# The opening of a fused recurrence and two-layer kernel in the order of one table: three plain blocks, the first two side by side

## The chip, the cores and the metric

The kernel runs on one core of one Trainium2 chip. The metric is the device time of one execution in microseconds (us), lower is better. Every run quoted here, of every kernel, was in the fast state, with a mean granted TensorE clock (the share of full speed that the profile lists) of 0.99 or more, so all of them may be compared. The time of a run is 1.7 to 1.9 us longer than the span of its profile (2.2 to 3.2 in the kernel turn_dve below), so times are set against times and spans against spans.

## The reference

A gated recurrence along the sequence is followed, for each token, by two matrix products with an elementwise function between them.

```python
# x, f_logit: (4, 6080, 256) float32, w_in: (256, 2048) and w_out: (2048, 256) float64
sig = 1 / (1 + np.exp(-f_logit))
f = lower_bound + (1 - lower_bound) * sig
for t in range(6080):                       # per batch row and channel
    h = f[:, t] * h + (1 - f[:, t]) * x[:, t]
    y[:, t] = h
x = y.reshape(24320, 256)
h = x @ w_in
out = ((h - np.tanh(h)) @ w_out).astype(np.float32)
```

The weights arrive as 64-bit floats. The kernel takes the words apart with integer operations and builds fp32 numbers ("rounding a weight", seven steps on VectorE and ScalarE). For small h, h - tanh(h) is a polynomial in h². A guard collects how large h became, and one branch at the end would run a slower fallback, `general()`; with these data it is skipped.

## The kernel before

The 24320 tokens are cut into blocks. The first blocks are "plain": ordinary fp32 matmuls, 32 of 128x512 and 64 of 128x256 for 512 tokens. All later blocks use seven products in place of eight for each 2x2 cut of a matrix product. For these, sums of the weight quarters and of the input quarters must exist first. In the steady part a fixed word list `around` puts the instructions of three neighbouring blocks into each engine's queue, and each engine works its queue off in that order (x_early below shows a wait that comes of it). Matmuls write into banks of PSUM, here of 128x512 fp32 numbers; a bank is free again when its content has been read.

```python
sizes = [TB] + [HB] * (N % TB // HB) + [TB] * (N // TB - 1)   # 512, 256, then 46 x 512
PLAIN = 1 + N % TB // HB                                      # 2: 512 and 256 are plain

def turn(j, s):                      # VectorE: tokens x channels -> channels x tokens
    nc.vector.transpose(
        out=dst[:, 0:n].rearrange("p j k b -> p (j k b)"),
        in_=nats[j, s][:, 0:n, :].rearrange("p j c -> p (j c)"))
def recur(j, k): ...                 # VectorE: tensor_tensor_scan of 128 channels

def to_float32(dsts, raw, temps): ...   # VectorE e, m, r, e, w; ScalarE r, e; all at once

def plain_first(j, u):               # first layer, a quarter u of the 2048 features
    # per half s: 4 matmuls into two PSUM banks (A A, then B D), ScalarE: square, quadratic,
    # VectorE: factor, two products that read the banks
def plain_second(j, u): ...          # second layer into banks Qa, Qb (or Qc)

# ... the opening, in this order in every queue
for step in REC:                     # the whole recurrence of block 0
    steps[step](0)
fetch(1)
ready(0)                             # rounds w_in of quarter 0
for u in range(NU):
    plain_first(0, u)
    for i in {0: (1, 2), 1: (3, 4), 2: (5, 6), 3: (7,)}[u]:
        ready(i)                     # rounds the next weights, two at a time
    if u > 0:
        plain_second(0, u - 1)
    for step in REC[3 * u : 3 * u + 3]:
        steps[step](1)
# ... the same for block 1, with sum_weight() between
bank = ps_b.tile([P, 2, HB], FP32, name="B", tag="B")
nc.tensor.matmul(bank[:], lhsT=zeros[:, 0:P], rhs=zeros[:], ...)   # "the dummy"
for cycle in range(PLAIN, NBLK + 3):
    for name, u, at in turns: ...    # the seven-product part
```

The **dummy**, a matmul of zeros, stands where the plain part ends and the seven-product part begins. I call that place the seam.

Of the kernel before, what the change touches and what calls it, by code (L numbers as in the profile page):

```python
# [7 lines left out]

# [8 lines left out]
P = 128  # L17
# [13 lines left out]
def kernel(  # L31
# [37 lines left out]
    assert D == 2 * P and DFF == 4 * TB and N % HB == 0  # L69


    sizes = [TB] + [HB] * (N % TB // HB) + [TB] * (N // TB - 1)
    PLAIN = 1 + N % TB // HB
# [12 lines left out]
    zeros = const.tile([P, TB], FP32, name="zeros")  # L86



    def fetch_w_in(u, raw, queue):  # L90

        src = moe_w_in.rearrange(
            "(i k a) (s u f) -> i k u a s f", i=G, k=KC, a=H, s=2, u=NU
        )
        dst = raw.rearrange("p (k s f) -> p k s f", k=KC, s=2)
        for i in range(G):
            for k in range(KC):
                queue.dma_start(out=dst[i * H : (i + 1) * H, k], in_=src[i, k, u])
# [8 lines left out]
    def to_float32(dsts, raw, temps):  # L107




        hi = raw.bitcast(INT32).rearrange("p (n c) -> p n c", c=2)[:, :, 1]
        lo = raw.bitcast(UINT32).rearrange("p (n c) -> p n c", c=2)[:, :, 0]
        e, m, r = [t.rearrange("p a b c -> p (a b c)") for t in temps]
        nc.vector.tensor_scalar(
            out=e.bitcast(INT32), in0=hi, scalar1=20, scalar2=0x7FF,
            op0=ALU.logical_shift_right, op1=ALU.bitwise_and,
        )
        nc.scalar.activation(out=r, in_=lo, func=AF.Copy, scale=2.0**-32)
        nc.scalar.activation(  # L120
            out=e.bitcast(INT32), in_=e.bitcast(INT32), func=AF.Relu,
            scale=float(1 << 23), bias=-896.0 * (1 << 23),
        )
        nc.vector.tensor_scalar(
            out=m.bitcast(INT32), in0=hi, scalar1=0xFFFFF, scalar2=0x100000,
            op0=ALU.bitwise_and, op1=ALU.bitwise_or,
        )
        nc.vector.tensor_tensor(out=r, in0=r, in1=m.bitcast(INT32), op=ALU.add)
        nc.vector.scalar_tensor_tensor(
            out=e.bitcast(INT32), in0=hi, scalar=-(1 << 31), in1=e.bitcast(INT32),  # L130
            op0=ALU.bitwise_and, op1=ALU.bitwise_or,
        )
        for dst, view in dsts:
            nc.vector.scalar_tensor_tensor(
                out=dst, in0=view(r), scalar=2.0**-20, in1=view(e),
                op0=ALU.mult, op1=ALU.mult,
            )

    def recurrence(ctx):
# [6 lines left out]
        def fetch(j):  # L146
            t0, nb = starts[j], sizes[j]
            for s in range(2):
                nat = natpool.tile([P, TB // H, KC * H], FP32, name=("fn", "xn")[s])
                src = srcs[s][t0 : t0 + nb, :].rearrange(  # L150
                    "(j b) (i c) -> i b j c", b=H, i=G
                )
                for i in range(G):
                    nc.sync.dma_start(
                        out=nat[i * H : (i + 1) * H, 0 : nb // H, :], in_=src[i]
                    )
                nats[j, s] = nat

        def turn(j, s):
# [5 lines left out]
                in_=nats[j, s][:, 0:n, :].rearrange("p j c -> p (j c)"),  # L165
# [57 lines left out]
        return fetch, steps, ys  # L223

    @with_exitstack
    def fast(ctx):
# [8 lines left out]
        fetch, steps, ys = recurrence(ctx)  # L235
# [17 lines left out]
        raws = {}  # L253

        def fetch_weight(n, queue):
            kind, u = n
            raw = rawpool.tile([P, KC * TB], INT64, name="raw")
            (fetch_w_in, fetch_w_out)[kind](u, raw[:], queue)
            raws[n] = raw

        def round_weight(n):
            kind, u = n
            raw = raws.pop(n)
            temps = [
                rawpool.tile([P, 2, 2, HB], FP32, name=s, tag=s, bufs=1)[:] for s in "emr"
            ]
            w = (w_in, w_out)[kind][u]
            if kind == 0:
                dsts = [(w[:, 0:4, :].rearrange("p n f -> p (n f)"), lambda a: a)]
            else:  # L270
                dsts = [
                    (
                        w[:, 2 * s + k, :].rearrange("p (n a) -> p n a", a=H),
                        lambda t, s=s, k=k: t[:, s * TB : (s + 1) * TB].rearrange(
                            "p (n k a) -> p n k a", k=2, a=H
                        )[:, :, k],
                    )
                    for s in range(2)
                    for k in range(2)
                ]  # L280
            to_float32(dsts, raw[:], temps)

        def sum_weight(n):
            kind, u = n
            w = (w_in, w_out)[kind][u]
            A21 = S3
            for o, a, b, op in (
# [3 lines left out]
                (S3, A11, A21, ALU.subtract),  # L291
            ):
# [174 lines left out]
        def give(j):  # L467
            n = sizes[j] // H
            osb = opool.tile([P, TB // H, KC, H], FP32, name="osb", tag="osb")
            nc.vector.transpose(  # L470
                out=osb[:, 0:n].rearrange("p j k a -> p (j k a)"),
# [7 lines left out]
            for i in range(G):  # L479
                nc.sync.dma_start(  # L480
                    out=dst[i],
                    in_=osb[i * H : (i + 1) * H, 0:n].rearrange("b j k a -> b j (k a)"),
# [61 lines left out]
        def plain_first(j, u):  # L544

            nb = sizes[j]
            n = j * NU + u
            gT = hpool.tile([P, 2, 2, TB], FP32, name="h", tag="h")
            st[n] = gT
            for s in range(2):  # L550
                banks = []
                for c in range(2):
                    pool, name = ((ps_a, "A"), (ps_b, "B" if c == 0 else "D"))[s]
                    bank = pool.tile([P, TB], FP32, name=name, tag=name)
                    banks.append(bank)
                    for k in range(KC):
                        nc.tensor.matmul(  # L557
                            bank[:, 0:nb],
                            lhsT=w_in[u][:, 2 * k + s, c * P : (c + 1) * P],
                            rhs=ys[j][:, k, 0:nb],  # L560
                            start=(k == 0),
                            stop=(k == KC - 1),
                        )
                t, q = [
                    tpool.tile([P, 2, TB], FP32, name=name, tag=name)[:, :, 0:nb]
                    for name in "tq"
                ]
                for c in range(2):
                    nc.scalar.activation(
                        out=t[:, c], in_=banks[c][:, 0:nb], func=AF.Square  # L570
                    )
                nc.scalar.activation(out=q, in_=t, func=AF.Square, scale=RA, bias=RB)
                nc.vector.scalar_tensor_tensor(  # L573
                    out=q, in0=q, scalar=RC, in1=t, op0=ALU.add, op1=ALU.mult
                )
                for c in range(2):
                    nc.vector.tensor_tensor(  # L577
                        out=gT[:, s, c, 0:nb], in0=banks[c][:, 0:nb], in1=q[:, c],
                        op=ALU.mult,
                    )  # L580
                junk = sumpool.tile([P, 2, TB], BF16, name="junk", tag="junk")
                nc.scalar.activation(
                    out=junk[:, :, 0:nb], in_=t, func=AF.Relu, bias=-TINY,
                    accum_out=flags[:, 2 * n + s : 2 * n + s + 1],
                )

        def plain_second(j, u):

            nb = sizes[j]
            ns = nb // P  # L590
            gT = st.pop(j * NU + u)
            if u == 0:
                acc[j] = [
                    ps_b.tile([P, 2, D], FP32, name=f"Q{b}", tag=f"Q{b}")
                    for b in ("ab" if j == 0 else "c")[0 : (ns + 1) // 2]
                ]
            for s in range(2):
                for c in range(2):
                    for i in range(ns):
                        nc.tensor.matmul(  # L600
                            acc[j][i // 2][:, i % 2].rearrange("p (k m) -> p k m", k=2),
                            lhsT=gT[:, s, c, i * P : (i + 1) * P],
                            rhs=w_out[u][:, 2 * s : 2 * s + 2, c * P : (c + 1) * P],
                            start=(u == s == c == 0 and i % 2 == 0),
                            stop=(u == NU - 1 and s == c == 1),
                            skip_group_check=True,
                        )
            if u == NU - 1:
                osb = opool.tile([P, NQ, D], FP32, name="osb", tag="osb")
                for i in range(ns):  # L610
                    nc.scalar.copy(
                        out=osb[:, i].rearrange("p (i k a) -> p k i a", k=2, a=H),
                        in_=acc[j][i // 2][:, i % 2].rearrange(
                            "p (k i a) -> p k i a", k=2, a=H
                        ),
                    )
                nc.sync.dma_start(
# [218 lines left out]
```

## Time and profile before

| | before |
|---|---|
| median of four runs | 2373.88 us (2373.49 to 2375.92) |
| span of the traced run | 2374.0 us |
| first matmul on the recurrence's output | 25.0 us |
| TensorE idle in the first 100 us | 40.4 us |
| TensorE idle from 1000 to 2000 us | 0 |

The head of the page of the kernel before gives each engine's busy time, its share of the span and its instructions:

```profile
span 2374.0 us, 28606 instructions
...
PE 2316.8 (98%) x10628; PEld 2020.9 (85%) x10628; DVE 2130.6 (90%) x2456; ACT 1801.3 (76%) x2685; POOL 2.5 (0%) x8
```

The 57 us in which TensorE (PE) is not busy are 2.4% of the span, nearly all in the first 150 us and in the last 12. So nearly all that order can gain lies in the opening, and the gain is bounded. The start of VectorE's (DVE) timeline of the kernel before (start, duration, engine, line, operation, output and inputs, count, and in brackets the idle time before and who ended it) shows what stands in the way:

```profile
14.63 1.25 DVE L163 STREAM_TRANSPOSE xT<-xn 128x1024 f32<-128x1024 f32 x1 [3.84 <-DMA xn<-in_x_dram]
...
18.81 1.22 DVE L207 TENSOR_TENSOR_SCAN y<-f,v 128x512 f32<-128x512 f32 x1
19.96 0.67 DVE L115 TENSOR_SCALAR e<-raw 128x1024 int32<-128x1024 int32 x1
```

VectorE waits 3.84 us for x, finishes the recurrence at 20.0, and only then touches a weight that ScalarE had begun to convert at 13.16. The queue's order, not the data, makes the weight late.

### The profile page before, as it was taken

The numbers are of one execution on the slowest core, as the hardware profiler recorded it, in microseconds if no ns is written. First come the engines' busy times: TensorE is split into PE (matmuls) and PEld (weight loads), VectorE is DVE, ScalarE is ACT, GpSimd is POOL, SyncE is SP. The second block draws the span as 40 slices with busy tenths as digits, with TensorE's granted clock in tenths as the row PEclk, the third lists the DMA queues.
The fourth block names the chain that finished last, engine by engine and source line by source line (L and its number), as shares of the span: only waits on it lengthen the run. The fifth ranks groups of instructions, "written<-read, shape, count | busy, mean of one in ns | idle before, by whom it ended". The sixth has DMA issues, their size and how long they took to land.

```text
span 2374.0 us, 28606 instructions
## 1 busy us (share of the span) xinstructions
PE 2316.8 (98%) x10628; PEld 2020.9 (85%) x10628; DVE 2130.6 (90%) x2456; ACT 1801.3 (76%) x2685; POOL 2.5 (0%) x8
## 2 busy tenths in 40 slices
PE   4999999999999999999999999999999999999997
PEld 2678888888888888888888888888888888888886
DVE  5888999899999999899989999899989999999987
ACT  4678777877777777777787777777787777777775
POOL 0000000000000000000000000000000000000000
PEclk9999999999999999999999999999999999999999
DMA  5321111211121111211121111111121112111101
GB/s 115 80 48 28 36 27 27 45 36 27 27 43 29 36 27 30 42 36 27 27 45 34 30 27 36 36 36 27 27 45 36 27 27 41 32 36 27 27 9 29
DMA packets 303669, 85.06 MB, mean 36 GB/s; under 512 B 298656, under 2 KB 299424, under 8 KB 303520
## 3 DMA queue, kind: packets, MB, share of 16 engines
q1 hardware_dynamic: 302752, 82.09, 16.9%
q8 instruction: 85, 1.39, 0.3%
q10 hardware_dynamic: 640, 1.05, 0.2%
q14 instruction: 64, 0.52, 0.1%
q0 software_dynamic: 128, 0.00, 0.0%
HBM read 58.20 MB, written 24.90 MB: 35 GB/s over the span
## 4 chain that ended last, share of the span: by engine, by line
PE 95%; DVE 2%; DMA 1%; ACT 1%; issue 0%; SPq 0%; DVEq 0%
PE A L350 26%; PE Qd L433 13%; PE Qb L433 13%; PE Qa L433 13%; PE D L350 13%; PE Qc L433 7%; PE B L350 7%; PE A L557 1%; DMA raw<-in_moe_w_in_dram 1%; PE Qb L600 0%; PE Qa L600 0%; DVE q L573 0%; DVE w_out L293 0%; PE D L557 0%; PE B L557 0%; DVE h L577 0%
## 5 line engine op out<-in xcount | busy, mean ns | idle before, releaser
L350 PE MATMUL A<-T,w_in 128*128 128x256 f32 x2208 | 559.2, 379 | 2.0 <-ACT r L362 1.8
L350 PEld LDWEIGHTS A<-T,w_in 128*128 128x128 f32 x2208 | 419.4, 190 | 59.7 <-ACT r L362 2.2
L394 DVE TENSOR_TENSOR h<-h,q 128x1024 f32<-128x1024 f32 x368 | 437.3, 1219 | 3.2
L388 DVE SCALAR_TENSOR_TENSOR q<-q,t 128x1024 f32<-128x1024 f32 x368 | 439.7, 1216 | 0.0
L381 ACT ACTIVATE q<-t 128x1024 f32<-128x1024 f32 x368 | 382.7, 1052 | 45.3 <-DVE h L394 42.4
L378 ACT ACTIVATE t<-h 128x1024 f32<-128x1024 f32 x368 | 388.6, 1056 | 4.8 <-DVE h L365 2.0
L399 ACT ACTIVATE junk<-t 128x1024 bf16<-128x1024 f32 x368 | 388.1, 1055 | 1.5
L413 DVE TENSOR_TENSOR Tg<-h 128x1024 f32<-128x1024 f32 x368 | 347.9, 945 | 6.5
L433 PE MATMUL Qb<-h,w_out 128*128 128x256 f32 x1472 | 347.7, 379 | 0.0
L433 PEld LDWEIGHTS Qb<-h,w_out 128*128 128x128 f32 x1472 | 279.7, 190 | 38.0
L433 PE MATMUL Qa<-Tg,w_out 128*128 128x256 f32 x736 | 218.9, 379 | 0.0
L433 PE MATMUL Qd<-h,w_out 128*128 128x256 f32 x736 | 218.9, 379 | 0.0
L433 PE MATMUL Qa<-h,w_out 128*128 128x256 f32 x736 | 218.9, 379 | 0.0
L433 PE MATMUL Qd<-Tg,w_out 128*128 128x256 f32 x736 | 218.9, 379 | 0.0
L362 ACT COPY h<-B 128x512 f32<-128x512 f32 x184 | 107.1, 582 | 144.8 <-PE B L350 94.9
L362 ACT COPY h<-A 128x512 f32<-128x512 f32 x184 | 107.3, 583 | 136.5 <-PE A L350 125.2
L365 DVE TENSOR_TENSOR h<-D,r 128x512 f32<-128x512 f32 x184 | 126.8, 689 | 90.7 <-PE D L350 89.7
L365 DVE TENSOR_TENSOR h<-A,r 128x512 f32<-128x512 f32 x184 | 126.2, 686 | 77.2 <-PE A L350 43.4
L350 PE MATMUL D<-T,w_in 128*128 128x256 f32 x736 | 189.1, 379 | 3.0 <-DVE T L320 1.6
L350 PE MATMUL A<-y,w_in 128*128 128x256 f32 x736 | 188.9, 379 | 0.0
L350 PE MATMUL B<-y,w_in 128*128 128x256 f32 x736 | 188.9, 379 | 0.0
L350 PE MATMUL D<-y,w_in 128*128 128x256 f32 x736 | 188.9, 379 | 0.0
(81 smaller groups left out, 2982.2 us busy)
## 6 DMA issues: line engine op xcount, KB each, us to landing
fn<-in_f_logit_dram SPq DMA_DIRECT2D x188, 128.0 KB, 3.1
xn<-in_x_dram SPq DMA_DIRECT2D x188, 128.0 KB, 3.3
out_dram<-osb SPq DMA_DIRECT2D x184, 128.0 KB, 2.8
raw<-in_moe_w_out_dram SPq DMA_DIRECT2D x8, 512.0 KB, 5.2
raw<-in_moe_w_in_dram SPq DMA_DIRECT2D x24, 128.0 KB, 3.4
raw<-in_moe_w_in_dram ACTq DMA_DIRECT2D x8, 128.0 KB, 5.0
out_dram<-osb SPq DMA_DIRECT2D x1, 512.0 KB, 3.0
fn<-in_f_logit_dram SPq DMA_DIRECT2D x4, 64.0 KB, 4.1
```

What stands on the lines that cost most here:

```text
L350: nc.tensor.matmul(ps[:, c], lhsT=w_in[u][:, slot, c * P : (c + 1) * P], rhs=mixes[j][right], start=start and c == 0, stop=True, skip_grou ...
L362: nc.scalar.copy(out=dst, in_=piece(n, bank))
L365: nc.vector.tensor_tensor(out=piece(n, "h")[:, q], in0=piece(n, bank), in1=piece(n, r), op=ALU.add)
L378: nc.scalar.activation(out=half(n, i, "t"), in_=half(n, i), func=AF.Square)
L381: nc.scalar.activation(out=half(n, i, "q"), in_=half(n, i, "t"), func=AF.Square, scale=RA, bias=RB,)
L388: nc.vector.scalar_tensor_tensor(out=q, in0=q, scalar=RC, in1=t, op0=ALU.add, op1=ALU.mult)
L394: nc.vector.tensor_tensor(out=h, in0=h, in1=q, op=ALU.mult)
L399: nc.scalar.activation(out=junk[:, :, :, 0 : st[n]["hb"]], in_=t, func=AF.Relu, bias=-TINY, accum_out=flags[:, 2 * n + i : 2 * n + i + 1],)
L413: nc.vector.tensor_tensor(out=o, in0=a, in1=b, op=ALU.subtract)
L433: nc.tensor.matmul(acc[j, part][:, r, 0 : st[n]["hb"]], lhsT=w_out[u][:, slot, c * P : (c + 1) * P], rhs=piece(n, right)[:, q, c], start=( ...
L557: nc.tensor.matmul(bank[:, 0:nb], lhsT=w_in[u][:, 2 * k + s, c * P : (c + 1) * P], rhs=ys[j][:, k, 0:nb], start=(k == 0), stop=(k == KC - 1),)
```

## The change

The intent is to shorten the opening. It has five parts, and some small ones.

- **Order by a table.** Every step of the opening is a word in one long string; the string's order is each engine's order. Rounding is spread in single steps.
- **Blocks.** Block 2 becomes plain too (512, 256, 512), and blocks 0 and 1 run side by side.
- **Turned by TensorE.** Blocks 0 and 1 are transposed by TensorE against an identity matrix; they then load in rows of 1 KB instead of 256 bytes.
- **Half a weight first.** The first 1 MB of w_in comes in two halves, each rounded alone.
- **Even and odd channels** are the two halves of the 256, in place of blocks of 32. A load of w_in then needs two transfers instead of eight, and VectorE's transposes read or write with a step of 8 bytes.
- **Small ones**, which no run here takes apart: three matmuls of zeros at the very start (TensorE is busy with them from 1.47 us for 5.49 us in after), lower_bound in one transfer instead of four, and the first loads spread anew over the queues of SyncE and ScalarE.

```diff
-    sizes = [TB] + [HB] * (N % TB // HB) + [TB] * (N // TB - 1)
-    PLAIN = 1 + N % TB // HB
+    sizes = [TB, HB] + [TB] * (N // TB - 1)
+    PLAIN, TURNED = 3, 2
...
-        for i in range(G):
-            for k in range(KC):
-                queue.dma_start(out=dst[i * H : (i + 1) * H, k], in_=src[i, k, u])
+        for s in range(2):
+            queue.dma_start(out=dst[:, :, s], in_=src[s, u])
...
-                in_=nats[j, s][:, 0:n, :].rearrange("p j c -> p (j c)"),
+                in_=nats[j, s][:, 0:n, :].rearrange("p j (a k) -> p j k a", k=KC),
...
+        order = [(0, 0, 0), (0, 0, 1), (0, 1), (1, 0), (0, 2), (1, 1), (0, 3), (1, 2), (1, 3)]
...
+                    nc.tensor.transpose(
+                        bank[:, i * P : (i + 1) * P], nats[j, s][:, i, k::2], ident[:],
+                    )
...
+        before = """
+            W.0 df.0 dx.0 ce.0 cr.0 cm.0 cx.0 W.1 cs.0 cb.0 tf.0 cw.0 df.1 W.2 tx.0 sg.0
+            f1.0 cm.1 ce.1 f0.0 v0.0 cx.1 cr.1 dx.1 cb.1 v1.0 W.3 sc0.0 tf.1 sc1.0 sg.1
+            f0.1 cs.1 f1.1 F.0.0.0 tx.1 df.2 cw.1 cm.2 cr.2 v1.1 v0.1 sc1.1 t.0.0.0
...
+            q.2.2.1 w.2.2.1 a.2.2.1 F.2.3.0 B.1.0 g.2.2.1 F.2.3.1 t.2.3.0 w.2.3.0
+            q.2.3.0 B.0.3 t.2.3.1 a.2.3.0 q.2.3.1 g.2.3.0 w.2.3.1 a.2.3.1 g.2.3.1
+        """
+        left = {
+            ("Qb", 1): ["S.2.1.0"],
...
+            ("Qd", 2): ["S.2.3.1", "B.1.1", "B.1.2", "B.1.3"],
...
+            for _ in range(3):
+                nc.tensor.matmul(
+                    bank[:], lhsT=zeros[:, 0:P], rhs=zeros[:], start=True, stop=True,
```

In the table, `W`, `df`, `dx` are loads of a weight, of f_logit, of x; `ce` to `cw` the rounding; `tf`, `tx` transposes; `sg`, `f0`, `f1`, `v0`, `v1` the sigmoid and the factors of the recurrence; `sc0`, `sc1` the two scans; `F.j.u.s` a first-layer group of matmuls and `S.j.u.s` a second-layer group; `t q a g w` the function between; `A` and `B` sums of weights; `m13`, `m2`, `m4` sums of the input quarters; `o` the output of a block. `left` names groups that are put into the first cycle after the seam.

> **What bounds the kernel now.** I read the page first, then stretches of busy time, then the waits and the chain of the first 160 us, then the timeline there. Busy time by stretch (us, then per engine busy us and instructions, granted clock, DMA share, GB/s; here PE, PEld, DVE, ACT, POOL):
>
> ```profile
> 0.00:100.00 100.00, 59.58 (x177) 36.12 (x178) 70.77 (x93) 49.50 (x69) 2.45 (x8) 0.93 0.50 110
> 100.00:150.00 50.00, 45.18 (x205) 38.20 (x205) 38.20 (x74) 27.71 (x60) 0.00 (x0) 1.00 0.28 59
> 1000.00:2000.00 1000.00, 1000.00 (x4635) 880.32 (x4634) 914.25 (x1038) 780.42 (x1159) 0.00 (x0) 1.00 0.16 33
> ```
>
> In the steady part TensorE never pauses (1000 of 1000 us), VectorE is 91% busy, ScalarE 78%. TensorE is the bound there, and only less work for it helps. The opening is another matter: 40 of the first 100 us have TensorE idle. The waits of TensorE up to 150 us (who waited for whom: us, times, longest):
>
> ```profile
> PE A L557 <- DVE w_in L134: 40.4, 4, 25.0
> PE A L350 <- ACT r L362: 1.8, 1, 1.8
> PE D L350 <- DVE T L320: 1.6, 1, 1.6
> PE D L350 <- DVE h L365: 1.4, 1, 1.4
> ```
>
> Its first matmul comes at 25.0 us, and three times more it waits for a weight to be rounded on VectorE (15.4 us together). Then 4.8 us go where the seven-product cycle fills. The chain in time order (start, duration) shows why the start is late, and what a matmul costs cold and warm:
>
> ```profile
> 12.15 5.03 DMA raw<-in_moe_w_in_dram
> 17.19 2.77 DMA fn<-in_f_logit_dram
> 19.97 0.66 DVE e L115
> ...
> 23.73 1.24 DVE w_in L134
> 25.00 5.89 PE A L557 x8
> 30.90 1.72 PE B L557 x4
> ...
> 80.95 5.23 PE A L557 x8
> ...
> 92.20 0.86 PE Qb L600 x4
> ```
>
> One fp32 matmul is two records. Four records of 128x512 take 1.72 us warm, of 128x256 0.86, so 0.43 and 0.216 each. Eight of 128x512 should take 3.45, but after a pause they took 5.89, 5.13, 5.40 and 5.23: 7.9 us lost to a cold clock. VectorE's order is the culprit: it does the whole recurrence of block 0, ending near 20 us, before it touches a weight.
>
> **Closing the sum for before.** A plain 512 block is 32 matmuls at 512 and 64 at 256: 64x0.4315 + 128x0.2157 = 55.2 us; the 256 block 27.6. A seven-product block is 112 matmuls, 224 records, 48.33 us. So 25.0 + 82.8 + 46x48.33 (2223.2) + 0.9 (dummy) + 15.4 + 4.8 + 7.9 + 12.1 (last matmul of work at 2361.9 to the end) = 2372.1 against 2374.0. The account is good to 2 us.
>
> **What the Trainium skill says.** (1) "TensorE: Matmul & The Clock Gate", Part 1: idle by default means half clock, some 3.4 us of activity lifts it. The trace agrees: 0.85 us a record at first, 0.43 later; even a 2.4 us pause (before 80.95) cost it. (2) "SBUF — State Buffer", section on the DMA port swizzle, note on 16-byte lines: two fp32 hits in a line keep full rate. The new even/odd split reads and writes with an 8-byte step. The trace agrees for reads: the rounding already takes every second 32-bit word, and 128x1024 of it takes 0.68 us, no slower than any contiguous op. No strided DVE write is shown. (3) "DMA: Bandwidth & Descriptors", Specifications: under 512 B a transfer is slower. Here the 256-byte rows of f_logit and x moved at about 190 GB/s, the weights' 2 KB rows alone at up to 397. (4) "ScalarE: Activation LUTs", What ACT_TABLE_LOAD costs: about 1283 ns; the trace has 1.28 us. The change has two, by its instruction order, where before has one.
>
> **The change part by part.**
> *More plain work.* Blocks are 512, 256, 512 plain and 45 with seven products: +55.2 - 48.3 = **+6.9 us** of TensorE. The opening's matmuls are then 138.0 us.
> *The start.* Half a w_in is fetched first (512 KB in 2 KB rows), with f on one queue and x on another in 1 KB rows. Data began to move at 2.0 us before; 1.5 MB at some 330 GB/s (an estimate between 190 and 397) has f here near 7.3, the weight near 6. ScalarE: r 0.65, e 0.65, table 1.28, ready near 8.6; TensorE has transposed f by then. Two sigmoids from PSUM (0.6 each) to 9.8, two f (0.67) to 11.2, e of the second half 11.8. VectorE in order: v, then cb waiting for that e, 12.5; v 13.2; two scans (1.27) to 15.8. **First real matmul at 16 us** (before 25.0): -9. It is cold, since TensorE pauses about 5 us after its transposes: +2.
> *Blocks 0 and 1 side by side.* x of block 1 is transposed on TensorE after that first group (at 21.2), and VectorE waits for it: two v (0.45), two scans (0.75), so F of block 1 starts near 24.4: 2.6 us idle. Next the first whole w_in: on VectorE from 24.3 ce 0.6, cs 1.2, a 1.2, cb 1.2, g 1.3, a 0.7, cw 1.24 = 31.8, just when TensorE has used up its 10.4 us of groups. Banks B and D come free at 37.4, TensorE is at 35.5: 1.9 idle. The second layer starts at about 40.9.
> *From there to the seven-product part.* I walked both queues with start-to-start times of before (1.15 to 1.2 for 1024 columns, 0.62 to 0.68 for 512, 5.0 for a rounding, 1.2 for three sums). VectorE stays 0 to 4 us ahead of what TensorE needs: about 123 us of VectorE, 100 of ScalarE against 138. I find only fractions of idle (0.6) until F of the third block runs out. There the dummy matmul needs bank B, which is read last after t 1.2, q 1.0, a 1.2, g 0.65: **4.3 us idle**. In the filling cycle six plain groups of 3.45 us are put in; 4.8 becomes about 2.
> *Steady part and tail.* Same order, same counts; the three transposes per block only change stride. Nothing.
>
> Sum: 16 + 138.0 + 0.9 + 45x48.33 (2174.9) + 12.1 = 2341.9; with 2 + 1 (cold, first and second gap), 0.5 (transposes between), 2.6, 1.9, 0.6, 4.3, 2 of waits, = 2356.8. The account of before was 2 short, and a tuned table may do a little better than my walk: **2356 us**, 18 under before. In differences: start -9, weight and bank waits 15.4 to 9.4 = -6, cold -5, filling -3, third plain block +7, rounded.
>
> **Rivals.**
> *The order works perfectly*: no idle after 16 us, no cold clock: 2342. For it: 15 us of VectorE room over the opening. Against it: queues are in order, and each group must go matmul, ScalarE, VectorE before its bank is free.
> *VectorE or ScalarE becomes the bound of the opening*, every wait of one hitting the other: ten more pauses of 1 to 2 us and colder clocks, 2368. For it: my slack is often under 1 us. Against it: the rounding is spread finely now, not as a 5 us block before each group.
> *Strided transposes are slower.* 3 of 1.24 us a block; doubled they would add 3.7 us to 44.2 of 48.3, 99% busy, and VectorE would begin to set the pace: 2380 to 2430. Against it: note (2). I give it 4%.
> *The start is transfer-bound*: lower_bound took 5 us to land before and VectorE stands in order behind it; if it lands at 8.3 again, all moves by 2.
>
> **Range and chances.** The start is good to 2 us, the waits I summed (12) to 5, cold clocks to 2, unmodelled coupling mostly upward: 2346 to 2367. Over 2% faster needs 2326.6, below the 2342 of the perfect case: 2%. Slower than 2421 only if the steady part breaks: 2%.
>
> **What would show each step.** First matmul on y near 16 us (right: 14 to 18). Idle of TensorE after it some 10 to 14 us up to the dummy, which I expect at 146. Largest single pause at that dummy. 1000 us of 1000 busy in the middle, transposes still 1.24 us. Two table loads of 1.28. Wrong if transposes lengthen, if weights land late, or if small pauses keep the clock cold through the first 40 us.

## The result

| | before | after |
|---|---|---|
| median of four runs | 2373.88 us | 2353.98 us |
| range | 2373.49 to 2375.92 | 2353.07 to 2354.64 |
| ratio, 95% interval | | 0.9914, 0.9897 to 0.9931 |

The change is 19.9 us by the medians, against 18 predicted; the time lies in the predicted range, and within 2% of before. The two traces differ by 21.7 us, because the traced run of before (2375.8 us) lay 1.9 above its median. The ratios in this document are the mean time of one kernel's fast runs over that of the other's of the same rounds, so not quite the ratio of the medians. The head of the page of the kernel after:

```profile
span 2352.3 us, 28494 instructions
...
PE 2329.0 (99%) x10626; PEld 2019.8 (86%) x10626; DVE 2105.5 (90%) x2437; ACT 1794.1 (76%) x2681; POOL 1.4 (0%) x7
```

TensorE is busy 12 us longer (the zero matmuls at the start add 5.5, the third plain block 6.9; the transposes add, and the milder cold clock takes away, some 3 each), and idle 34 us less: 23 in place of 57. The waits of TensorE up to 160 us of the kernel after (waiter, releaser, us in total, times, longest) are the answer to the four weight waits of before:

```profile
PE B L825 <- DVE h L682: 4.0, 1, 4.0
PE A L644 <- DVE y L227: 3.8, 1, 3.8
PE Qa L644 <- DVE y L227: 2.4, 1, 2.4
...
PE B L644 <- DVE h L682: 1.0, 1, 1.0
```

No wait for a weight is left. The second row is before the first group on y, the third before block 1's first group, the last at bank B, and the first, the longest, at the dummy. Busy time by stretch of the kernel after (columns as in the prediction):

```profile
40.00:100.00 60.00, 60.00 (x240) 45.31 (x239) 57.12 (x89) 38.16 (x67) 0.00 (x0) 1.00 0.30 70
100.00:150.00 50.00, 46.03 (x143) 28.51 (x142) 34.53 (x52) 31.23 (x51) 0.00 (x0) 0.93 0.33 58
...
1000.00:2000.00 1000.00, 1000.00 (x4635) 880.32 (x4634) 914.61 (x1039) 782.51 (x1161) 0.00 (x0) 1.00 0.16 33
```

From 40 to 100 us TensorE never pauses, though VectorE is 95% busy beside it. Then 4 us are lost once more, and the granted clock falls to 0.93. The chain around that place in the kernel after (start, duration) shows the loss at the seam:

```profile
139.98 1.14 DVE q L676
141.15 0.70 DVE h L682
141.89 2.08 PE B L825 x2
143.97 1.71 PE A L383 x4
145.68 1.71 PE D L383 x4
147.38 1.06 PE Qa L706 x4
```

The dummy waits for VectorE to read bank B (`h`). After it four records of 128x256 take 1.71 us, twice the 0.86 of the warm clock. The pause of 3.97 us at the dummy has cooled it, and 2.08 + 1.71 + 1.71 + 1.06 = 6.56 us pass where 3.44 would do. The timeline of TensorE in the kernel after has the same for the first group on y:

```profile
14.44 5.40 PE L644 MATMUL A<-y,w_in 128*128 128x512 f32 x8 [3.83 <-DVE y L227]
...
22.75 1.10 PE L644 MATMUL Qa<-y,w_in 128*128 128x256 f32 x4 [2.45 <-DVE y L227]
```

Eight records took 5.40 us, where a warm group of this shape reads 3.60 in this view (3.45 from start to start). The 2.45 us pause cost nearly nothing (1.10, warm 1.03); in other traces a pause of this length did cost something, see two_plain and layout_alone. The groups by form show the strided transposes and the table loads of the kernel after (busy us, mean ns of one), which the prediction had at 1.24 and 1.28 us:

```profile
L183 DVE STREAM_TRANSPOSE fT<-fn 128x1024 f32<-128x1024 f32 x46 | 57.1, 1241 | 0.0
...
L503 DVE STREAM_TRANSPOSE osb<-C 128x1024 f32<-128x1024 f32 x45 | 55.8, 1240 | 0.0
...
L138 ACT ACT_TABLE_LOAD x1 | 1.3, 1283 | 1.2 <-PEq L960 1.2
L613 ACT ACT_TABLE_LOAD x1 | 1.3, 1283 | 0.0
```

The kernel before has 1235 and 1237 ns for the same two transposes: the step of 8 bytes costs 0.2 to 0.5% of an instruction that is not on the path.

### The profile page after: what moved, and what is told of

Read it like the earlier page. It is cut to its first block, busy times and chain, and to the rows that moved or that the text cites. A ratio compares the mean times of both kernels' runs of the same rounds, so it can differ in the third digit from the quotient of the medians.

```text
span 2352.3 us, 28494 instructions
## 1 busy us (share of the span) xinstructions
PE 2329.0 (99%) x10626; PEld 2019.8 (86%) x10626; DVE 2105.5 (90%) x2437; ACT 1794.1 (76%) x2681; POOL 1.4 (0%) x7
## 4 chain that ended last, share of the span: by engine, by line
PE 98%; DVE 1%; DMA 0%; ACT 0%; issue 0%; DVEq 0%; POOLq 0%
PE A L383 26%; PE D L383 13%; PE Qd L466 13%; PE Qa L466 13%; PE Qb L466 13%; PE B L383 7%; PE Qc L466 7%; PE A L644 1%; PE Qa L706 1%; PE Qb L706 1%; PE B L644 1%; PE Qc L706 1%; PE D L644 1%; DVE q L676 0%; DMA lb<-in_lower_bound_dram 0%; DVE h L682 0%
## 5 line engine op out<-in xcount | busy, mean ns | idle before, releaser
L383 PE MATMUL A<-T,w_in 128*128 128x256 f32 x2160 | 547.0, 379 | 0.0
L383 PEld LDWEIGHTS A<-T,w_in 128*128 128x128 f32 x2160 | 410.3, 190 | 56.1 <-ACT B L395 0.3
L427 DVE TENSOR_TENSOR h<-h,q 128x1024 f32<-128x1024 f32 x360 | 428.1, 1221 | 3.1
L421 DVE SCALAR_TENSOR_TENSOR q<-q,t 128x1024 f32<-128x1024 f32 x360 | 430.5, 1217 | 0.0
L414 ACT ACTIVATE q<-t 128x1024 f32<-128x1024 f32 x360 | 374.4, 1053 | 44.3 <-DVE h L427 41.5
L411 ACT ACTIVATE t<-h 128x1024 f32<-128x1024 f32 x360 | 380.2, 1056 | 5.3 <-DVE h L398 2.6
L432 ACT ACTIVATE junk<-t 128x1024 bf16<-128x1024 f32 x360 | 379.7, 1055 | 1.5
L446 DVE TENSOR_TENSOR Tg<-h 128x1024 f32<-128x1024 f32 x360 | 340.7, 946 | 6.4
L466 PE MATMUL Qb<-h,w_out 128*128 128x256 f32 x1440 | 340.2, 379 | 0.0
L395 ACT COPY r<-A 128x512 f32<-128x512 f32 x180 | 104.9, 583 | 105.1 <-PE A L383 105.1
```

What stands on the lines that cost most here:

```text
L383: nc.tensor.matmul(ps[:, c], lhsT=w_in[u][:, slot, c * P : (c + 1) * P], rhs=mixes[j][right], start=start and c == 0, stop=True, skip_grou ...
L395: nc.scalar.copy(out=dst, in_=piece(n, bank))
L411: nc.scalar.activation(out=half(n, i, "t"), in_=half(n, i), func=AF.Square)
L414: nc.scalar.activation(out=half(n, i, "q"), in_=half(n, i, "t"), func=AF.Square, scale=RA, bias=RB,)
L421: nc.vector.scalar_tensor_tensor(out=q, in0=q, scalar=RC, in1=t, op0=ALU.add, op1=ALU.mult)
L427: nc.vector.tensor_tensor(out=h, in0=h, in1=q, op=ALU.mult)
```

## The experiments

Twelve kernels ran in three batches (the third on another chip), each in five rounds beside the kernel before, which leaves four or five timed runs of each. All gave correct results. The column "less" is the mean of the kernel before in the same rounds minus the kernel's mean. The kernel after, run again unaltered, tells how far batches agree.

| kernel | batch | median us | less | ratio, 95% interval |
|---|---|---|---|---|
| after, as first measured | | 2353.98 | 20.4 | 0.9914, 0.9897 to 0.9931 |
| again (after, unaltered) | 3 | 2353.57 | 21.3 | 0.9911, 0.9897 to 0.9925 |
| seam_fill | 1 | 2348.16 | 25.6 | 0.9891, 0.9876 to 0.9906 |
| keep_warm | 1 | 2353.88 | 20.3 | 0.9915, 0.9901 to 0.9928 |
| x_early | 1 | 2351.04 | 22.2 | 0.9907, 0.9892 to 0.9922 |
| turn_dve | 1 | 2356.49 | 17.3 | 0.9927, 0.9913 to 0.9940 |
| two_plain | 2 | 2342.52 | 32.1 | 0.9863, 0.9848 to 0.9878 |
| layout_alone | 2 | 2371.83 | 3.0 | 0.9986, 0.9972 to 0.9999 |
| round_ahead | 2 | 2368.09 | 6.4 | 0.9971, 0.9958 to 0.9985 |
| all_three | 2 | 2345.41 | 29.1 | 0.9876, 0.9861 to 0.9891 |
| whole_first | 3 | 2356.28 | 18.2 | 0.9925, 0.9912 to 0.9938 |
| two_early | 3 | 2339.48 | 35.6 | 0.9852, 0.9839 to 0.9865 |
| two_early_warm | 3 | 2338.41 | 36.5 | 0.9847, 0.9834 to 0.9860 |

### again: how far two batches agree

No edit.

> The changed kernel once more, unaltered, as the measure for the other runs of this call: 2354, within 1 us.

It measured 2353.57 us (2353.00 to 2354.47), 0.4 us from the first time. Differences between kernels of different batches are good to about 1 us. Its trace shows one thing more. The dummy has the same pause of 3.97 us before it as in after, but the clock came back sooner (chain of the traced run of again):

```profile
142.61 2.07 PE B L825 x2
144.68 1.35 PE A L383 x4
146.03 0.86 PE D L383 x4
146.89 0.86 PE Qa L706 x4
```

These four steps took 5.14 us, 1.7 more than the warm 3.44, where after lost 3.1. So what the cold clock costs at the seam differs from execution to execution of one kernel.

### seam_fill: a group of matmuls ahead of the dummy

The theory: the loss at the seam is a pause plus a cold clock, and a group that is ready (`S.2.1.0`, 3.45 us) can stand in it. The rival: it is wanted in the first cycle, and its place there becomes a new wait.

```diff
-            q.2.3.0 B.0.3 t.2.3.1 a.2.3.0 q.2.3.1 g.2.3.0 w.2.3.1 a.2.3.1 g.2.3.1
+            q.2.3.0 B.0.3 t.2.3.1 a.2.3.0 q.2.3.1 g.2.3.0 w.2.3.1 a.2.3.1 g.2.3.1 S.2.1.0
...
-            ("Qb", 1): ["S.2.1.0"],
```

> The changed kernel with one plain group of the third block (8 second-layer matmuls, 3.45 us) moved ahead of the dummy matmul, into the 4.0 us pause there. My theory: the pause at the dummy falls from 4.0 to about 0.5 us, the clock stays warm, so the matmuls after it no longer lose 3.1 us: 6 us less than the changed kernel's 2354.0, about 2348. Rival: the filler is missed inside the seven-product cycle and the wait comes back there: at most 3 us less, 2351 or more.

It took 5.8 us off the time of after by the medians, 5.2 by "less". Waits up to 160 us and then the timeline of TensorE in this kernel:

```profile
PE B L824 <- DVE h L682: 0.5, 1, 0.5
```

```profile
142.74 1.12 PE L824 MATMUL B<-zeros 128*128 128x512 f32 x2 [0.52 <-DVE h L682]
143.70 1.03 PE L383 MATMUL A<-y,w_in 128*128 128x256 f32 x4
```

The pause fell from 3.97 to 0.52 us, and the four records after the dummy take 1.03 us in this view, the warm figure. 3.45 us of pause and 3.1 of clock are 6.6; 5.2 to 5.8 came out, which fits a cold clock that costs 1.7 us in one trace and 3.1 in another. In the cycle after the seam no new wait appeared. The theory held: the group of plain matmuls in `left` was on the wrong side of the dummy.

### keep_warm: zero matmuls in the pause before the first group

```diff
+        def p_zero():
+            for _ in range(4):
+                nc.tensor.matmul(warm[0][:], lhsT=zeros[:, 0:P], rhs=zeros[:], ...)
...
-  sc0.0 tf.1 sc1.0
+  sc0.0 tf.1 z sc1.0
```

> The changed kernel with four more zero matmuls (3.4 us warm) in the 3.8 us pause between the transposes and the first matmul on y. Theory of the cold clock: the first eight records go from 5.40 us to about 3.7 (a wait for the second scan stays), and everything after moves with them: 1.7 us less, 2352.3. Rival: the group is stretched by the wait for the scan and by VectorE behind it, not by the clock: no change (under 0.5 us).

The trace shows what was meant, in the timeline of TensorE:

```profile
14.52 3.96 PE L644 MATMUL A<-y,w_in 128*128 128x512 f32 x8 [0.42 <-DVE y L227]
```

The first eight records took 3.96 us instead of 5.40. But the times fell by 0.1 by the medians and not at all against the kernel before. This is not resolved. The cold group is not the same length in every execution: in traced runs where a pause of 3.8 to 3.9 us stands before it, it took 5.40, 6.09, 6.03 and 6.58 us (after, seam_fill, again, two_plain). One trace of each kernel cannot say how long it is on average.

### x_early: x of block 1 before the first group

The pause of 2.45 us comes because TensorE turns block 1's x only after its first group, so VectorE stands still meanwhile, 3.01 us in after. The next word of its queue that needs nothing new is `ce.2`, whose weight `cm.2` had read at 16.73 us, but it stands behind and runs at 22.52. Here both are done before.

```diff
-  W.0 df.0 dx.0 ce.0
+  W.0 df.0 dx.0 dx.1 ce.0
...
-  f0.1 cs.1 f1.1 F.0.0.0 tx.1 df.2
+  f0.1 cs.1 f1.1 tx.1 F.0.0.0 df.2
```

> The changed kernel with x of block 1 fetched right after x of block 0 and transposed ahead of the first matmul group instead of after it. My theory (VectorE waits 3.0 us for these transposes, TensorE 2.45 us for block 1's y): that pause goes and the first group is not later: 2.4 us less, 2351.6. Rival: the transfer moved forward pushes the second half weight back by 0.25 MB, 0.7 us, and the start with it: 1.5 us less or nothing.

It measured 2.9 us less than after by the medians, 2.3 by the means (one of its four runs was at 2353.82). The timeline of TensorE:

```profile
15.12 4.88 PE L644 MATMUL A<-y,w_in 128*128 128x512 f32 x8 [0.43 <-DVE y L227]
...
20.33 1.10 PE L644 MATMUL Qa<-y,w_in 128*128 128x256 f32 x4 [0.32 <-DVE y L227]
```

The first group starts 0.7 us later, and block 1's group 2.4 us earlier, with 0.32 us of pause. The dummy moved from 141.89 to 139.48. The pause was due to the order of the table and could be had back.

### two_plain: no third plain block

The prediction charged 6.9 us for the third plain block. The theory: nothing needs it. The rival: it buys the time in which VectorE makes the sums for the seven-product part (`A`, `B`), and without it the seam stalls.

```diff
-    PLAIN, TURNED = 3, 2
+    PLAIN, TURNED = 2, 2
...  # all plain steps of block 2 leave the table, its recurrence stays, fetch(PLAIN + 1) goes; after g.1.3.1 come
+            m13.2 A.0.0 m2.2 B.0.0 m4.2 A.0.1 A.1.0 B.0.1 A.0.2 A.1.1 B.0.2 A.0.3 B.0.3
+            A.1.2 A.1.3 B.1.0
...
+            ("Qd", 2): ["B.1.1", "B.1.2", "B.1.3"],
```

> The changed kernel with two plain blocks instead of three (46 seven-product blocks as before); the third block's plain steps leave the table, the sums of the weights follow the last plain group. My theory: the third plain block costs 6.9 us of TensorE and is not needed: TensorE ends its plain work near 104 us, VectorE its sums near 108, and the filling of the seven-product cycle costs 5 to 8 us of waits against the 7.1 (pause and cold clock) of the seam now. Sum 104 + 2223 + 6 + 12: 2345, 2342 to 2350. Rival, the change's own idea: VectorE needs the third block's time for its sums; without it TensorE waits 8 us or more, so 2354 or slower.

It took 11.5 us off the time of after by the medians (11.7 by "less"). The waits of TensorE up to 160 us and then its timeline in this kernel:

```profile
PE A L644 <- DVE y L227: 3.8, 1, 3.8
...
PE Qa L644 <- DVE y L227: 2.4, 1, 2.4
PE B L644 <- DVE h L682: 0.7, 1, 0.7
PE A L383 <- ACT r L395: 0.2, 1, 0.2
```

```profile
105.81 1.02 PE L811 MATMUL B<-zeros 128*128 128x512 f32 x2
106.67 1.03 PE L383 MATMUL A<-y,w_in 128*128 128x256 f32 x4
```

The dummy has no pause before it, the clock is warm, and only 0.2 us of waiting follows in the seven-product part. Three costs of the third block went together: 6.9 us of matmuls, 4.0 of pause and 3.1 of cold clock, 14.0 in sum. The fall is 2 to 3 us less than that. The trace shows where it went, in the timeline of TensorE:

```profile
23.97 2.04 PE L644 MATMUL Qa<-y,w_in 128*128 128x256 f32 x4 [2.44 <-DVE y L227]
```

The pause before block 1 is the one of after, but here the clock was cold behind it: the groups into Qa and Qb took 3.37 us from start to start, in after 1.80. With the first group, 1.2 us longer than in after (6.58), that is 2.8 us, and 14.0 less 2.8 is near the 10.7 us by which the two spans differ.

### layout_alone: even and odd channels in the kernel before

```diff
-                in_=nats[j, s][:, 0:n, :].rearrange("p j c -> p (j c)"),
+                in_=nats[j, s][:, 0:n, :].rearrange("p j (a k) -> p j k a", k=KC),
...
-                out=osb[:, 0:n].rearrange("p j k a -> p (j k a)"),
+                out=osb[:, 0:n].rearrange("p j (a k) -> p j k a", k=KC),
...  # and the same order of channels in both weights, lower_bound and the stores
```

> The kernel before with the even and odd channels as the two halves and nothing else (w_in in 2 transfers per part instead of 8, lower_bound in one, transposes and output with the 8-byte step). My theory: the steady part is unchanged (1000 of 1000 us busy, transposes 1.24 us), the start gains from fewer transfers: first matmul at 21 to 23 us instead of 25.0, total 2370 to 2372. Rival: the layout itself is worth more in the opening through faster weight transfers: 2366 or less; or the strided transposes cost: 2378 or more.

It gained 3.0 us. The first matmul came at 24.1 us, 0.9 earlier, where 2 to 4 had been expected; the transposes took 1238 to 1241 ns. The two traces differ by 4.0 us: 0.9 at the start, 1.9 at the very end, and 1.2 in between. Those 1.2 are mostly one group of matmuls that met a cold clock in before and a warm one here, behind equal pauses (timelines of before and of this kernel), so they say nothing of the layout:

```profile
80.95 5.23 PE L557 MATMUL A<-y,w_in 128*128 128x512 f32 x8 [2.38 <-DVE w_in L134]
```

```profile
80.53 3.70 PE L552 MATMUL A<-y,w_in 128*128 128x512 f32 x8 [2.38 <-DVE w_in L131]
```

At the end it is this. After the flag is copied (2364.92 us in before, 2362.82 here) the trace of before goes on for 9.1 us and this one for 7.2. SyncE's own waits from 2325 us on have the reason, for the kernel before and then for this one; the line is that of the branch over `general()`:

```profile
SPq L802 <- SPq L802: 5.2, 3, 3.0
```

```profile
SPq L793 <- SPq L793: 3.4, 2, 3.1
```

Three waits became two, in six of the other traces with the new layout only one; their sums are 2.7 to 3.4 us there and 5.2 in both traces with the old one. All twelve traces with the new layout end 7.0 to 7.2 us after the flag, and both with the old one (before and round_ahead) 9.1. The fallback that is jumped over contains the same weight loads, now two transfers in place of eight. That its length is what shortens the jump is likely, not shown.

### turn_dve: the first two blocks transposed by VectorE

```diff
-    PLAIN, TURNED = 3, 2
+    PLAIN, TURNED = 3, 0
```

> The changed kernel with blocks 0 and 1 fetched in 256-byte rows and transposed on VectorE as before; the table is the same. My theory: the first matmul on y moves from 14.4 to 18 to 20 us, and VectorE has 3.9 us more to do in the part where it is nearly full: 4 to 7 us more, 2358 to 2361. Rival: where the turning is done does not matter, the order does: at most 2 us more.

It is 2.5 us slower than after by the medians. By the median spans it is 1.8; the rest lies outside the span and stays open. The timeline of TensorE:

```profile
17.13 5.94 PE L644 MATMUL A<-y,w_in 128*128 128x512 f32 x8 [11.28 <-DVE y L227]
```

The first group comes 2.7 us later, and the dummy at 144.11 is 2.2 later than in after. So the start moved by 2.7 and nothing more was lost: the 3.9 us that VectorE now spends on transposes hide in its slack. The result lies between the theory (4 to 7) and the rival (at most 2). TensorE's transposes are worth the start alone; the run changes the rows of the loads with them, so it doesn't tell the two apart.

### whole_first: the first weight in one piece

```diff
-        order = [(0, 0, 0), (0, 0, 1), (0, 1), ...
+        order = [(0, 0), (0, 1), ...
...  # the table without the steps of the second half, later weights renumbered
```

> The changed kernel with the first w_in part fetched and rounded whole (1 MB) instead of in two halves. Theory: the halves matter by when f_logit lands behind them and by VectorE's free time ahead of the recurrence: first matmul 1.5 to 2 us later, 2355.5 to 2356. Rival: the first group waits for y only, so the halves buy nothing: within 0.5 us.

It is 2.7 us slower by the medians than the repeat of after in the same batch. The first group starts at 16.27 instead of 14.44 us: f_logit lands 1.5 us later behind the larger load, and the sigmoid stands in ScalarE's queue behind a longer conversion. The timeline of ScalarE (ACT) shows one thing more:

```profile
7.68 1.28 ACT L138 ACT_TABLE_LOAD   x1 [7.68 <-DMA raw<-in_moe_w_in_dram]
```

The first table load ran only when the weight had landed; in after it ran at 1.21 us, before any data. So part of the delay may be this load and not the size of the weight; the run doesn't tell them apart. The loss is a little more than expected.

### round_ahead: the order of before with weights rounded one step earlier

This asks how much of the gain the order of the rounding alone would give, without blocks side by side.

```diff
             ready(0)
+            ready(1)
             for u in range(NU):
                 plain_first(0, u)
-                for i in {0: (1, 2), 1: (3, 4), 2: (5, 6), 3: (7,)}[u]:
+                for i in {0: (2, 3), 1: (4, 5), 2: (6, 7), 3: ()}[u]:
```

> The kernel before with each w_in part rounded one stage earlier on VectorE, ahead of the group that runs before it; no other change. My theory: the three later waits for w_in (15.4 us) are a matter of VectorE's order alone, so they shrink to some 4 us and with them the cold clocks: 10 us less, 2364. Rival: only block 1 beside block 0 gives VectorE the time: at most 4 us less, 2370 or more.

It gained 6.4 us, between the 10 of the theory and the 4 of the rival. The waits of TensorE up to 160 us in this kernel:

```profile
PE A L557 <- DVE w_in L134: 24.3, 1, 24.3
PE A L557 <- DVE h L577: 7.5, 4, 3.9
...
PE Qa L600 <- DVE w_out L134: 1.7, 2, 1.4
```

The three later weight waits of before, 15.4 us, are gone. 7.5 us of waiting for VectorE to read bank A and 1.7 for w_out have come in their place. With one block at a time TensorE waits for banks that VectorE has still to read. In after such a wait is left once before the seam (1.0 us), so it seems that the matmuls of block 1 fill these gaps; no run takes the two blocks apart under the new order.

### all_three, two_early, two_early_warm: the findings together

```diff
# all_three: seam_fill + x_early + two zero matmuls after tf.1
# two_early: two_plain + x_early
# two_early_warm: two_early + two zero matmuls after tf.1
```

> The changed kernel with all three mends: the plain group in the seam, x of block 1 early, and two zero matmuls in the pause before the first group. The single runs gave 5.8, about 2.5 and about 0.3 us by device time (1.4 by the trace). If they are independent: 2345 to 2346. Rival, that mends at the start are eaten by VectorE before the seam: 2347 to 2348.

> Two plain blocks, with x of block 1 fetched and transposed early. Theory: the 2.45 us pause for block 1's y goes here too: 2342.7 less 2.4 is 2340.3. Rival: TensorE then runs into VectorE's sums and the gain is lost at the seam: 2342 or more.

> As two_early, with two zero matmuls ahead of the early transposes, so that the first group runs at the full clock. Theory: 1 us less than two_early, 2339.3. Rival, from the run with four zero matmuls that gained 1.4 us in its trace and 0.3 us in the times: no difference that can be told from noise.

All three came out within about 1 us of what was expected: 2345.41, 2339.48 and 2338.41 us. The gains of the seam and of x_early add. The zero matmuls gave 1.1 us in two_early_warm by the medians; its five runs lie within 0.5 us of each other, those of two_early within 1.8. That fits a cold group whose length varies, but the traces of both kernels show the first group at 3.96 us (that of two_early is of its fastest run, 2338.35), so it is not shown. two_early_warm is the fastest kernel of this study: 15.6 us under after by the medians, and 36.5 us under before by the means of the same rounds.

## Why the prediction was right

The predicted time was 2356, the measured 2353.98. Here is its sum again, term by term, with the trace of after beside it.

| term of the prediction | predicted us | trace of after us |
|---|---|---|
| first matmul on y | 16 | 14.44 |
| plain matmuls, dummy, 45 blocks | 2313.8 | 2313.8 by the same formula |
| last matmul of work to the end | 12.1 | 9.9 |
| cold clock, first and second group | 3 | 2.0 |
| transposes of block 1 in between | 0.5 | 0.5 |
| pause before block 1 | 2.6 | 2.45 |
| pause at bank B | 1.9 | 1.0 |
| fractions | 0.6 | 0 |
| pause at the dummy | 4.3 | 3.97 |
| filling of the cycle | 2 | 3.1, but of another kind |
| sum | 2356.8 | 2351.2 (span 2352.3) |

The account of after is 1.1 us short of the trace, as that of before was 2.

That the number came so near is partly luck. The prediction closed its account of before on the span, and on the span its sum of 2356.8 was 4.5 us too long: nearly every term was taken a little too high. And its own terms don't give the 18 us: 2356.8 against its account of before, 2372.1, is 15.3 less. The 18 comes of setting off the 2 us by which the account of before was short against a table that "may do a little better than my walk", which is a guess. The measured 19.9 is 1.9 from the number, but 4.6 from what the terms add up to.

- **The bound and the opening: right.** The steady part is unchanged, 1000 of 1000 us with 4635 records in both. The gain is all in the opening and the end.
- **The start: right in mechanism, 1.6 us off.** The step that failed is "two scans (1.27) to 15.8". The scans began at 13.16 us, where the working had 13.2. But the first matmul needs the first scan alone; the second ends 1.1 us after that, while TensorE works. The working had waited for both.
- **Pauses: right.** The three after the start were found where they had been placed, in the right order of size, none off by more than 0.9 us. The largest is the one at the dummy, as forecast. Two of the signs that it named are missed all the same: 10 to 14 us of idle time up to the dummy (7.4, and its own terms add up to 9.4), and the dummy at 146 (141.89). x_early and seam_fill took away one each, and gained about what it had cost.
- **Filling of the cycle: wrong kind.** "4.8 becomes about 2" was meant as waits. There were none after the dummy. What cost 3.1 us was the cold clock behind the 4 us pause that the prediction itself had named. It had charged the cold clock at two pauses and not at the largest. seam_fill shows it: with the pause gone the clock was warm.
- **The tail: wrong.** "Steady part and tail ... Nothing" overlooked 2.1 us at the branch. layout_alone shows that they belong to the layout.
- **The third plain block: right in size, wrong in worth.** +6.9 us of matmuls is what it adds. Unasked in the prediction was whether it is needed. two_plain shows that it is not, and that it brings the pause at the seam with it.
- **The rivals.** Perfect order (2342) failed for the change as written; two_plain comes to 2342.5, but by leaving out 6.9 us of work. VectorE as the bound of the opening failed: TensorE paused 7.4 us in all after its start. Strided transposes failed at 1240 ns. The late lower_bound failed: VectorE had it at 6.35 us, 0.2 after ScalarE began on the weight.
- **A reading that doesn't hold.** The 190 GB/s for the 256-byte rows are from stretches in which a weight moved too; from 5 to 10 us 0.76 of the 1.00 MB were w_in's. No run here shows these rows alone. The estimate of the start didn't suffer: f_logit was there at 7.80 us, for 7.3 in the working.

On the cold clock, the Trainium skill ("TensorE: Matmul & The Clock Gate", Part 1) says that the window in which activity is watched runs freely, so that the number of cold matmuls differs from run to run. The traces agree: a first group of 5.40 to 6.58 us after pauses of one length. That would be why keep_warm could not be resolved, and any prediction of this term is uncertain by 1 us and more.

Where the 20 us came from, by the traces of before and after: start 25.0 to 14.44, -10.6 (turn_dve: 2.7 of it by TensorE's transposes, whole_first: 1.8 by the half weight, the late table load among it, layout_alone: 0.9 by the layout; these may overlap, and the rest was not isolated); later pauses 15.4 to 7.4, -8.0; filling 4.8 to 0; cold clock 7.9 to 5.1, -2.8 (uncertain by 1 us and more, as the other traces show); tail -2.1; third block +6.9; block 1's transposes +0.5. The sum is -20.9; the spans differ by 21.7, the medians by 19.9.

## What to carry to other kernels

Where each engine works its queue in order, look for the step that needs nothing new and still comes late because it stands behind others in a queue: moving the rounding of the weights one step ahead was worth 6.4 us alone, and no instruction became faster for it. When you place filler work at a change of phase, put it before the pause and not after it, since a pause of 4 us was paid a second time as a cold clock. And ask of each added piece of work what would happen without it: the third plain block cost 11 us, and without it no wait at the seam was longer than 0.2 us.

## What the Trainium skill lacked or had wrong

- "TensorE: Matmul & The Clock Gate", section "Why this matters for your kernels", advises no gaps of more than some 3 us. A gap below that was not always free: behind 2.38 us the same eight records took 5.23 us in before and 3.70 in layout_alone (warm 3.60), and behind 2.4 us a group took 2.04 us in two_plain and 1.10 in after (warm 1.03). Gaps of 3.8 to 4.0 us cost 1.7 to 3.1 us each (5.40 to 6.58 us for 3.45, and 5.14 to 6.56 for 3.44 at the seam). The page has no figure for gaps shorter than the window.
- The same page, Part 4 (PE-mode transpose): it gives 275 to 390 ns for one of 128x128 in bf16. Here four in fp32 into one bank start 0.48 us apart from the next four, so 0.12 us each in a row, and 0.85 us apart in whole_first and all_three, where the granted clock was 0.50. It also says that transposes do not count as busy for the clock; x_early (0.43 us of pause after transposes, then 4.88 us) agrees, two_early (0.63, then 3.96) does not, so it stays open.
- "ScalarE: Activation LUTs", What ACT_TABLE_LOAD costs: the 1283 ns agree. The further 1380 ns of a drain do not show: the operation before the load ended at 7.58 us and the sigmoid began at 8.89, 1.31 us in all.
- "SBUF — State Buffer", the note on 16-byte lines: the rule holds, also for VectorE's writes of a transpose with an 8-byte step, for which the note gives no figure: 1240 ns against 1237.
- "Runtime: NRT & Kernel Launch", Instruction fetch mechanics: it says that a taken branch to a far target must fetch first, without a figure. Here SyncE waited 5.2 us in all at the branch over the fallback in before and 2.9 in after; that these waits are such a fetch is not shown.
